# One attention visit per pair of heads instead of two, beside a feed-forward that holds TensorE

## The chip, the cores and the metric

The kernel runs on one core of a Trainium2 chip. The metric is the device time of one execution in microseconds (us); lower is better. A core has a matrix engine (TensorE, PE in the profile), a vector engine (VectorE, DVE), an activation engine (ScalarE, ACT), a general engine (GpSimd, POOL) and an engine that in this kernel only issues transfers (SyncE, SP). Each works through its own instructions in the order in which they were written; semaphores make one engine wait for another. Matmul results land in eight PSUM banks; all other tiles are in SBUF.

## The reference

Attention with normalised queries and keys, for 8 batches, 12 heads, 448 positions and 64 dimensions per head, and then a feed-forward on the 3584 tokens that come out of it:

```python
def rmsnorm(x, g):
    rms = np.sqrt(np.mean(x * x, axis=-1, keepdims=True) + 1e-06)
    return x / rms * g
q_n, k_n = (rmsnorm(q, g_q), rmsnorm(k, g_k))
scores = scale * np.matmul(q_n, k_n.transpose(0, 1, 3, 2))
scores = scores - np.max(scores, axis=-1, keepdims=True)
attn = np.exp(scores)
attn = attn / (np.sum(attn, axis=-1, keepdims=True) + 1e-09)
x = np.matmul(attn, v)            # then (B,H,S,D) -> (B*S, H*D) = (3584, 768)
h = np.maximum(x @ w_in, 0.0)     # w_in 768 x 2048
out = (h * h @ w_out)             # w_out 2048 x 768
```

All matmuls are in float32. The two weight matrices come in as 64-bit floats, and the kernel turns their words into float32 on the chip.

## The kernel before

**Pairs.** The 96 heads are worked through in 48 pairs, `i` = 0 to 47, six pairs for each batch. The two heads of a pair (`e` = 0 and 1) lie on partitions 0 to 63 and 64 to 127. The 448 keys of a head are cut into slots `m`: three of 128 keys, and the 64 last ones. The last keys of an even and an odd pair share one slot, `m == NJ` (3), which is computed with the even pair. So an even pair has four slots and an odd one three.

For each slot `weigh` (L378) makes the scores of both heads (L387, two matmuls on different halves of the array's rows, four for the shared slot) in two PSUM banks, and takes their exponentials on ScalarE (L392) into tiles `wT`, of which there are eight. `attend` (L446) multiplies a slot's exponentials by the values and accumulates in bank 4 (L455, two matmuls on different halves of the array's columns). The sums of the exponentials are added up on GpSimd (`additions`, L411) and brought over the partitions by one more pair of matmuls (`denominators`, L485), which writes the bank of `sums_bank` (bank 3 for these pairs); VectorE turns that bank (`take_sums`, L496), inverts (`invert`, L505 to L512) and multiplies bank 4 by it (`finish`, L524).

The queries and keys of a pair are loaded by `load_qk`, squared on ScalarE (L179), added up on VectorE (L192, L195), raised to the power -1/2 and scaled on GpSimd (`rescale`, L201 and L216), stored and loaded back in blocks of 32 by 32 (`store_q` L303, `load_blocks` L319), and transposed on VectorE (`turn_blocks`, L328, and L330 on ScalarE for the queries).

**Feed-forward.** Two batches make one pass `ffn(u)`, `u` = 0 to 3. Each product of halves is made by a seven-product scheme. A pass has four blocks. A block has two sets of seven first products (L643, six profile records of a 128x448 matmul for each product; ScalarE copies L650, VectorE adds L663, ScalarE squares L664 and L665), then the tokens left over (L695), then three sets of seven second products (L724, VectorE accumulates them, L765 and L741). Each product adds `COST_IN` (18) or `COST_OUT` (10) to `spent`; a block is 502, a pass (`COST`) 2008. A float32 matmul has two records in the profile.

**Order.** All engines follow an order written out by hand (`manual_schedule`). Pairs 0 to 12 run alone (`visit_alone`). From pair 13 on `run(until)` issues feed-forward products until `spent` reaches a mark, and `visit_among(i, n)` puts attention between them. A pair has two visits there:

- visit 0: the first two slots of the values of pair `i - 1`, then slots 0 and 1 of pair `i`;
- visit 1: the `denominators` and the other two slots of the values of pair `i - 1`, then the other slots of pair `i`.

In pass 0 (`first`) the `denominators` are put by themselves into the feed-forward, halfway between two visits. Small pieces of other work stand in two lists, `tasks` and `pool_tasks`; `run_tasks` takes one or two of each after every product, and all of them before a visit.

**Weights.** The 64 pieces of the weights are converted by `convert`: three ScalarE instructions (L825 to L827) on a tile `words`, of which there are three, and three VectorE ones (L838, L858, L862), then sums of pieces by VectorE and GpSimd in turn (L884). The first 16 pieces, for block 0, are converted beside the pairs that run alone. The other 48 are converted in pass 0, when `spent` reaches the entries of `late`: for block `b + 1`, eight pieces of `w_in` from halfway through block `b` on, and eight of `w_out` in the first half of block `b + 1`. Passes 1 to 3 load finished forms.

## Time and profile before

| | us |
|---|---|
| median of 5 runs | 1461.14 |
| lowest and highest of them | 1460.86, 1462.84 |
| the profiled execution's own time | 1461.48 |
| its span | 1459.7 |
| TensorE busy | 1425.5 |
| VectorE, ScalarE, GpSimd busy | 667.0, 583.7, 623.0 |

The span is the time from the first to the last instruction in the profile; 1.78 us of the profiled execution's time lie outside it. The stages follow the order above: pairs 0 to 12 alone until 147.4 us, pass 0 of the feed-forward with attention and conversion of weights until 511.6 us, passes 1 and 2 with attention until 1198 us, and then the rest of the feed-forward alone. Busy time of TensorE is a union of modelled spans, so a wait shorter than a matmul's drain does not show as idle time: distances between starts say more.

### The profile page before, as it was taken

The page shows a single profiled execution, that of the slowest core. Times are in us where ns is not written, and L with a number is a line of the kernel's source. Part 1 is how long each engine was busy: PE and PEld are TensorE (multiplying, and loading weights), DVE is VectorE, ACT ScalarE, POOL GpSimd, SP SyncE. Part 2 cuts the span into 40 slices and gives each one's busy share as a digit, 9 for nine tenths or more (in the row PEclk, how much of TensorE's full clock was granted, in tenths as well). Part 3 has the DMA queues.
Part 4 walks back from the last instruction along what each step waited for, and adds up shares of the span by engine and source line. Part 5 has one row for each costly group of instructions (what it writes and reads, how often), then busy time and mean ns, then how long its engine had stood idle before and what let it go on. Part 6 is the DMA issues. An engine that isn't in the chain of part 4 may idle for free.

```text
span 1459.7 us, 15299 instructions
## 1 busy us (share of the span) xinstructions
PE 1425.5 (98%) x4932; PEld 680.5 (47%) x4932; DVE 667.0 (46%) x1269; ACT 583.7 (40%) x1102; POOL 623.0 (43%) x522
## 2 busy tenths in 40 slices
PE   6989999999999999999999999999999999999998
PEld 2323444444444444445454544445444455555554
DVE  5877356786777623324342542324334251132313
ACT  6764455747555144432514234342332403222130
POOL 4545745655555635353543545245342422021111
PEclk9999999999999999999999999999999999999999
DMA  6565336666657554444435464334523223223122
GB/s 149 163 203 138 76 85 179 169 188 165 197 173 220 161 169 103 136 114 132 116 66 165 117 185 126 108 97 99 169 64 111 82 104 135 87 76 124 38 87 79
DMA packets 309278, 188.11 MB, mean 129 GB/s; under 512 B 265796, under 2 KB 293316, under 8 KB 300996
## 3 DMA queue, kind: packets, MB, share of 16 engines
q1 hardware_dynamic: 308384, 186.84, 43.7%
q8 instruction: 41, 0.67, 0.2%
q14 instruction: 49, 0.40, 0.1%
q10 hardware_dynamic: 804, 0.20, 0.1%
HBM read 144.57 MB, written 42.40 MB: 128 GB/s over the span
## 4 chain that ended last, share of the span: by engine, by line
PE 90%; DVE 4%; issue 2%; POOL 1%; ACT 1%; SPq 1%; DMA 0%; POOLq 0%; DVEq 0%
PE bank L643 35%; PE bank L724 29%; PE bank L455 9%; PE bank L387 8%; PE bank L695 5%; PE bank L485 2%; PE bank L468 1%; POOL rr L201 1%; DVE few L505 1%; DVE out_sb L884 0%; DMA qk<-in_k_dram 0%; DVE inverse L512 0%; DVE acc L765 0%; POOL qk L216 0%; POOL acc L181 0%
## 5 line engine op out<-in xcount | busy, mean ns | idle before, releaser
L643 PE MATMUL bank<-xT,in_sb 128*128 128x448 f32 x1344 | 517.5, 543 | 0.0
L643 PEld LDWEIGHTS bank<-xT,in_sb 128*128 128x128 f32 x1344 | 251.8, 190 | 262.3 <-issue 250.2
L765 DVE TENSOR_TENSOR acc<-acc,bank 128x384 f32<-128x384 f32 x324 | 173.7, 549 | 278.9 <-PE bank L724 205.6
L392 ACT ACTIVATE wT<-bank,rr 128x448 f32<-128x448 f32 x288 | 161.1, 631 | 268.9 <-PE bank L387 248.9
L201 POOL TENSOR_TENSOR rr<-ms,minus_half 128x16 f32<-128x16 f32 (+3 forms) x50 | 125.7, 2514 | 332.9 <-DVE ms L195 304.2
L724 PE MATMUL bank<-out_sb,hid 128*128 128x384 f32 x768 | 267.4, 488 | 0.0
L663 DVE TENSOR_TENSOR hid<-bank,part 128x448 f32<-128x448 f32 x128 | 76.8, 621 | 306.1 <-PE bank L643 306.1
L724 PE MATMUL bank<-out_sb,sums 128*128 128x384 f32 x576 | 204.0, 490 | 3.4 <-DVE acc L765 3.3
L724 PEld LDWEIGHTS bank<-out_sb,hid 128*128 128x128 f32 x768 | 144.9, 190 | 106.9 <-issue 6.8
L411 POOL TENSOR_TENSOR sum<-sum,wT 128x448 f32<-128x448 f32 (+1 forms) x144 | 164.2, 1163 | 12.8 <-ACT wT L392 10.4
L387 PE MATMUL bank<-qT,kT 64*128 64x448 f32 (+1 forms) x768 | 164.0, 573 | 3.7 <-ACT qT L330 1.6
L679 POOL TENSOR_TENSOR sums<-hid 128x384 f32<-128x384 f32 x32 | 32.8, 1024 | 291.5 <-ACT hid L665 291.0
L664 ACT ACTIVATE hid<-hid 128x448 f32<-128x448 f32 x128 | 73.2, 572 | 201.2 <-DVE hid L663 201.2
L724 PEld LDWEIGHTS bank<-out_sb,sums 128*128 128x128 f32 x576 | 107.7, 190 | 87.9 <-DVE acc L765 8.4
L650 ACT COPY part<-bank 128x448 f32<-128x448 f32 x128 | 67.7, 529 | 180.9 <-PE bank L643 180.8
L455 PE MATMUL bank<-wT,vt 128*64 128x448 f32 x480 | 106.3, 547 | 0.0
L387 PEld LDWEIGHTS bank<-qT,kT 64*128 64x128 f32 (+1 forms) x768 | 55.2, 173 | 108.8 <-issue 91.4
L411 POOL TENSOR_TENSOR sum<-wT 128x448 f32<-128x448 f32 x72 | 83.8, 1182 | 45.9 <-PE bank L485 45.9
L192 DVE TENSOR_REDUCE ms<-squares 128x8 f32<-128x512 f32 (+1 forms) x68 | 41.9, 616 | 124.7 <-ACT squares L179 124.7
L695 PE MATMUL bank<-out_sb,hid 128*128 128x384 f32 x256 | 86.4, 491 | 0.0
L665 ACT ACTIVATE hid<-hid 128x448 f32<-128x448 f32 x128 | 73.8, 577 | 4.0
L695 PEld LDWEIGHTS bank<-out_sb,hid 128*128 128x128 f32 x256 | 47.7, 190 | 39.3 <-issue 5.7
(83 smaller groups left out, 1126.4 us busy)
## 6 DMA issues: line engine op xcount, KB each, us to landing
out_sb<-out_forms SPq DMA_DIRECT2D x24, 1536.0 KB, 7.7
in_sb<-in_forms SPq DMA_DIRECT2D x24, 1344.0 KB, 6.0
words<-in_moe_w_in_dram SPq DMA_DIRECT2D x32, 384.0 KB, 3.6
words<-in_moe_w_out_dram SPq DMA_DIRECT2D x32, 384.0 KB, 3.7
out_forms<-out_sb SPq DMA_DIRECT2D x8, 1536.0 KB, 6.9
in_forms<-in_sb SPq DMA_DIRECT2D x8, 1344.0 KB, 5.5
qk<-in_q_dram SPq DMA_DIRECT2D x96, 96.0 KB, 3.1
vt<-in_v_dram SPq DMA_DIRECT2D x96, 96.0 KB, 3.3
```

The lines of the kernel that those rows point to most:

```text
L201: self.nc.gpsimd.tensor_tensor(out=self.rr[i][:, first : first + number, 0 : self.count(i)], in0=ms, in1=self.minus_half[:, :, None].to_br ...
L387: nc.tensor.matmul(sc[some], lhsT=turned[p, 1][r, keys], rhs=turned[p, 0][r, :], start=True, stop=True,)
L392: nc.scalar.activation(new_weights((i, m), e), sc, AF.Exp, scale=rows.rr[i][:, 1, 2 * m + e : 2 * m + e + 1],)
L411: nc.gpsimd.tensor_tensor(out=sums[i, e][some], in0=left[some], in1=weights[key_of(i, m), e][some], op=ALU.add)
L455: nc.tensor.matmul(banks[4][ds(e * D, D), 0:S], lhsT=lasts[i % 2][mine, e, :] if m == NJ else values[i][:, m, e, :], rhs=weights[key_of(i, ...
L643: nc.tensor.matmul(ps, lhsT=w_sb[:, IN.index(left), c, :], rhs=forms[u, c][right], start=first and c == 0, stop=c == NK - 1, skip_group_ch ...
L663: nc.vector.tensor_tensor(out=dst, in0=left, in1=right, op=op)
L664: nc.scalar.activation(dst, dst, AF.Relu)
L665: nc.scalar.activation(dst, dst, AF.Square)
L695: nc.tensor.matmul(ps, lhsT=flat[a][:, t, ds(NT * P, P)], rhs=w_sb[t][:, 2 * a + half, :], start=(a, t) == parts[0], stop=(a, t) == parts[-1],
L724: nc.tensor.matmul(ps, lhsT=lefts[left][:, t, ts(tt, P)], rhs=w_sb[t][:, OUT.index(right), :], start=first and t == 0, stop=t == 1, skip_g ...
L765: nc.vector.tensor_tensor(out=acc, in0=acc, in1=ps, op=ALU.add)
```

## The change

From pair 13 on each pair has one visit instead of two. Its order on TensorE: the scores of slots 0 and 1 of pair `i`; the four slots of the values of pair `i - 1`; the `denominators` of pair `i - 1` where they have not been made; the scores of the other slots of pair `i`. The exponentials of slots 0 and 1 are written between the value matmuls, since their tiles come free one slot at a time.

`weigh` is split into `score` (matmuls) and `weigh` (exponentials). The banks are dealt differently: slots 0 and 1 use banks 0 to 3, slot 2 banks 1 and 2, the shared slot banks 3 and 0, and the sums bank becomes bank 0. In pass 0 the `denominators` keep a place of their own, three quarters of the way from one visit to the next, and all waiting tasks are issued before them. Squares, normalisation and the turn through memory are made for pair `i + 3` instead of `i + 2`, so pair 12 prepares both 14 and 15; the transposes of pair `i + 1` and the loads of pair `i + 4` are put into `tasks` halfway before visit `i`. Pass 0 begins with five products ahead of pair 13's visit instead of two. The times of `late` change: pieces of `w_in` from 0.4 of block `b` on, 0.06 of a block apart, pieces of `w_out` from the start of block `b + 1` on, 0.055 apart.

The order of the instructions up to pair 11, and the number of matmuls, exponentials and transfers, stay as they are.

```diff
-    def weigh(i, m):
-
-        scs = [banks[m % 2 * 2 + e][:, 0:S] for e in range(2)]
+    def banks_of(i, m):
+
+        first = m % 2 * 2 if m < 2 or i <= 2 * NPAIR else 1 + (m - 2) * 2
+        return [banks[(first + e) % 4][:, 0:S] for e in range(2)]
+
+    def score(i, m):
+
+        scs = banks_of(i, m)
         for p in (i, i + 1) if m == NJ else (i,):
...
+    def weigh(i, m):
+
+        for e, sc in enumerate(banks_of(i, m)):
             nc.scalar.activation(
                 new_weights((i, m), e), sc, AF.Exp,
...
     def sums_bank(i):
-        return banks[5 if alone(i) else 3][:, 0:S]
+        return banks[5 if alone(i) else 0][:, 0:S]
...
     early = deque(2.4 * n for n in range(ahead + 1))
-    every = block / ahead
     late = deque(
-        block + 2 + every * (n - 2 * tile_pieces) for n in range(len(all_pieces) - ahead)
+        block * (n // ahead) + (0.4 * block + 0.06 * block * (n % ahead) if n % ahead < ahead // 2
+                                else block + 2 + 0.055 * block * (n % ahead - ahead // 2))
+        for n in range(len(all_pieces) - ahead)
     )
...
-    VISITS, last = 2, len(pairs) - 1
-    unit = 2 * NPAIR * VISITS
+    last, unit = len(pairs) - 1, 2 * NPAIR
...
     def visit_alone(i, n):
-        step = i * 2 * VISITS + 2 * n
+        later = (i + 2,) if alone(i) else (i + 2, i + 3)
+        step = 4 * i + 2 * n
...
-            square(i + 2, 0, new_acc())
-            square(i + 2, 1, new_acc(), nc.gpsimd)
+            for p in later:
+                square(p, 0, new_acc())
+                square(p, 1, new_acc(), nc.gpsimd)
...
-            normalize(i + 2)
+            for p in later:
+                normalize(p)
...
-    def visit_among(i, n):
+    def visit_among(i):
         run_tasks(len(tasks) + len(pool_tasks))
-        if not shift:
-            if n and i - 1 not in inverse:
+        if shift:
...
+        else:
+            if i <= last:
+                for m in slots_of(i, 0):
+                    score(i, m)
+            for n in range(NJ + 1):
+                attend(i - 1, (n,))
+                forget(i - 1, (n,))
+                if i <= last and n < 2:
+                    weigh(i, n)
+            if i - 1 not in inverse:
                 denominators(i - 1)
-            attend(i - 1, (2 * n, 2 * n + 1))
-            forget(i - 1, (2 * n, 2 * n + 1))
...
+            if i <= last:
+                weigh_slots(i, 1)
             tasks.append(lambda: invert(i - 1))
             tasks.append(lambda: finish(i - 1))
-        if n and i <= last and not shift:
-            additions(i)
...
+        if i <= last:
+            load_v(i)
+            if not shift:
+                additions(i)
+        if i + 3 <= last:
+            room = []
+            tasks.append(
+                lambda: room.append(io.tile([P, 4 * P], F32, name="squares", tag="squares", bufs=1))
+            )
+            for x in range(2):
+                tasks.append(lambda x=x: square(i + 3, x, room[0]))
+                tasks.append(lambda x=x: rows.add(i + 3, x))
+            tasks.append(lambda: pool_tasks.append(lambda: put_in_order(i + 3)))
...
+    def turn_among(i):
+        for x in (1, 0):
+            if in_blocks(i):
+                tasks.append(lambda x=x: turn_blocks(i, x))
...
         for i in range(len(pairs) + 1):
-            for n in range(VISITS):
-                at = i * VISITS + n - VISITS - unit
...
+            if i <= unit:
+                for n in range(2):
                     visit_alone(i, n)
-                    continue
...
+            u, x = divmod(i - unit - 1, unit)
+            if x == 0:
+                u, x = u - 1, unit
+            run(COST * (2 * x - 1) / (2 * unit))
+            if i < last and u >= 0:
+                turn_among(i + 1)
+            tasks.append(lambda i=i: load_qk(i + 4))
+            if first and u >= 0 and not shift:
+                run(COST * (4 * x - 1) / (4 * unit))
+                run_tasks(len(tasks) + len(pool_tasks))
+                denominators(i - 1)
+            run(COST * x / unit)
+            if x == unit:
+                drain()
+                stream, spent, first = ffn(u + 1), 0, u < 0
...
+                elif first:
+                    run(COST / (2 * unit))
+            visit_among(i)
+            if u < 0:
+                turn_among(i + 1)
```

## The prediction

> **What bounds the kernel now.** I read the page first (busy shares), then the table of stages, then TensorE's timeline in one stretch of each stage, then ScalarE's and VectorE's timelines where TensorE waits. Page, first part, and the table of stages (us from the start, PE, PEld, DVE, ACT, POOL busy, granted clock, DMA share, GB/s):
>
> ```profile
> PE 1425.5 (98%) x4932; PEld 680.5 (47%) x4932; DVE 667.0 (46%) x1269; ACT 583.7 (40%) x1102; POOL 623.0 (43%) x522
> 240.00:331.00 91.00, 88.61 (x294) 40.63 (x292) 71.50 (x120) 52.43 (x102) 51.84 (x40) 1.00 0.60 172
> 598.00:685.00 87.00, 87.00 (x299) 41.66 (x297) 32.66 (x64) 29.98 (x57) 38.71 (x32) 1.00 0.43 118
> ```
>
> TensorE is the bound: 98% busy, and from 511 us on it never idles; the clock is full. So only two things can shorten the span: less time per matmul, or the waits before 511 us, in pass 0, where VectorE is busy 71.5 of 91 us. The number of matmuls is the same. Time per matmul is not constant, as TensorE's timeline of the last stage (feed-forward alone) and of passes 1 and 2 shows (start, length, what, number of records):
>
> ```profile
> 1198.10 31.73 PE L643 MATMUL bank<-xT,in_sb 128*128 128x448 f32 x84
> 1229.67 5.32 PE L695 MATMUL bank<-out_sb,hid 128*128 128x384 f32 x16
> ...
> 699.80 11.54 PE L643 MATMUL bank<-xT,in_sb 128*128 128x448 f32 x30
> 711.27 0.97 PE L455 MATMUL bank<-wT,lasts 128*64 128x448 f32 x4
> 712.07 0.92 PE L455 MATMUL bank<-wT,vt 128*64 128x448 f32 x4
> 712.93 1.77 PE L387 MATMUL bank<-qT,kT 64*128 64x448 f32 x8
> 714.63 9.29 PE L643 MATMUL bank<-xT,in_sb 128*128 128x448 f32 x24
> 723.85 0.97 PE L485 MATMUL bank<-sum,ones 128*64 128x448 f32 x4
> 724.65 1.67 PE L455 MATMUL bank<-wT,vt 128*64 128x448 f32 x8
> 726.25 2.27 PE L387 MATMUL bank<-qT,kT 64*128 64x448 f32 x12
> ```
>
> From start to start, 84 uninterrupted records take 1229.67 - 1198.10 = 31.57 us, 0.3758 each. The 30 between two visits take 11.47, not 11.28: 0.20 over. The 24 take 9.22, not 9.02: 0.20 over. Two half-array matmuls run at once, so 8 value records should take 4 x 0.3758 = 1.50; they take 1.66: 0.15 over. 8 score records take 1.70: 0.20 over. Sums and values, both on halves of the columns, take 0.80 + 1.60 against 2.25: 0.15 over for both together. So **each stretch of one form costs 0.20 us (feed-forward, scores) or 0.15 us (values with or without sums), whatever its length**.
>
> **Part 1: fewer stretches.** Before, a pair has two stretches of each form: 2 x 0.20 + 2 x 0.20 + 2 x 0.15 = 1.10. After, scores, values with sums, scores, one feed-forward stretch: 0.20 + 0.15 + 0.20 + 0.20 = 0.75. That is 0.35 less, for the 35 pairs 13 to 47: 12.25. The visit behind the last pair has only values and sums, once instead of twice: 0.35 more. Pass 0 has sums by themselves 12 times instead of 11 (2.25 / 3 aside, such a stop costs 0.15 and one more feed-forward stretch, 0.20): 0.35 back. **Sum: 12.25 us.** One row is missing: feed-forward followed by scores. Nearest are feed-forward followed by values and scores followed by feed-forward (0.20 both), and transposes followed by scores or values (0.10); I take 0.20, which gives 12.25; with 0.10 it would be 15.75, with 0.25 10.5.
>
> [...]
>
> **Part 2: waits inside the visit.** Time from the visit's start, by the rows above: scores 0 to 1.70; values to 1.70 + 8 x 0.3758 + 0.15 = 4.85; with sums 5.60; then the other scores, into banks 1 and 2, which exponentials 2 and 3 must have read. An exponential of slot 0 needs its scores and one of the eight `wT` tiles, which the first value slot frees. ScalarE starts 1.1 us after the first start of what it waits for (scores at 626.86, exponentials at 627.97, four in 2.21), so at about 2.75; the third ends at 2.75 + 2 x 0.52 + 0.63 = 4.42. Slack: 1.1 us with sums in the visit (passes 1 and 2), 0.35 without (pass 0). Behind a late score stand all feed-forward products, in TensorE's order. For even pairs the shared slot also needs bank 0 after L496: sums end at 5.67, the transpose takes 0.64, the matmul comes at 6.45: nothing to 0.2 us each; I take 0. If VectorE had a backlog there, that would show 1:1.
>
> In passes 1 and 2 ScalarE is free in time (the nearest row before the visit, the square of the hidden values, ends 2.0 us into it), so I take no wait. In pass 0 three visits follow the tenth product of a block, with a conversion (L825) ahead of the exponentials in ScalarE's order. At the same place before, TensorE and ScalarE:
>
> ```profile
> 267.79 1.72 PE L455 MATMUL bank<-wT,vt 128*64 128x448 f32 x8
> ...
> 270.51 0.56 ACT L825 ACTIVATE words<-words 128x384 f32<-128x384 f32 x1 [4.05 <-DVE out_sb L884]
> 272.02 0.56 ACT L664 ACTIVATE hid<-hid 128x448 f32<-128x448 f32 x1
> 273.10 2.19 ACT L392 ACTIVATE wT<-bank,rr 128x448 f32<-128x448 f32 x4
> ```
>
> The exponentials start 5.31 us after the visit's start; in the next blocks 3.46 (361.13 - 357.67) and 4.16 (454.77 - 450.62). Before, nobody waited for them. After, that is 2.56, 0.71 and 1.41 over 2.75, less 0.35: 2.2 + 0.35 + 1.05 = 3.6 us. The changed order puts transposes (2 x 0.64), L496 and two joins (L838, L858, L862: 0.57 + 0.75 + 1.00) between the block's seventh and tenth product on VectorE, some 7.9 us with L884, after 1.35 us of adds, against 7.7 of TensorE; the tenth product's add is then 1.6 us late, which gives about 1.8 a visit, 5.4. I take **4.5** (0 to 9).
>
> **Part 3: waits of pass 0.** Before, TensorE waits at two places:
>
> ```profile
> 253.05 1.92 PE L387 MATMUL bank<-qT,kT 64*128 64x448 f32 x8
> 255.42 0.97 PE L387 MATMUL bank<-qT,kT 64*64 64x448 f32 x4 [0.45 <-ACT qT L330]
> ...
> 292.77 1.56 PE L724 MATMUL bank<-out_sb,sums 128*128 128x384 f32 x4 [0.68 <-DVE acc L765]
> 295.58 1.56 PE L724 MATMUL bank<-out_sb,sums 128*128 128x384 f32 x4 [1.25 <-DVE acc L765]
> ```
>
> The first: the shared slot needs the next pair's turned queries. From start to start these 12 records take 2.95, 3.27, 2.16, 3.52 and 3.26 us in pass 0, 1.87 where nothing is late: 5.8 us. After, the transposes are issued a quarter of a pair before the visit at the latest, from blocks loaded a pair earlier, and the shared slot comes 6 us into the visit: **5.8 us gone**; late next is what part 2 counts. The second: the 20 records of second products ahead of the visit take 9.01, 8.41 and 7.04 us instead of 6.54: 4.8 us. VectorE has more to do there than TensorE gives it time for, two conversions and their sums among it. The new `late` leaves about as many, and adds the two transposes and L496 for L511 to L524: I keep **4.8** (0 to 10). At the start, the sums of pair 13 come two products after its visit: six additions on GpSimd of 1.13 us end about when TensorE gets there: 0.3 (0 to 3).
>
> **Part 4: moved at no cost.** Pair 12 squares and scales pair 15 too: GpSimd 0.83 + 2.27 + 0.83 us; the first feed-forward products that need its T3 and T4 are the sixth and seventh, behind the visit of pair 13. SyncE: 9 more issues there (0.5 us each), all loads of q and k half a pair earlier, `load_v` behind the visit; each is used a pair (28 us) later and lands in 3.3. If a load came late, ScalarE's squares would hold up its copies (L650): up to some us once, in the range.
>
> **The sum.** Span 1459.7 - 12.25 - 5.8 - 4.8 + (4.5 + 4.8 + 0.3) = 1446.4. The profiled execution took 1461.48, 1.78 more than its span, and the median is 0.34 lower: 1446.4 + 1.78 - 0.34 = **1448**.
>
> **Rivals.** (A) Slower: the second scores wait for the exponentials of the first in every visit. For it: the chain scores, values, exponentials, scores exists only now, with 0.35 or 1.1 us of slack. Against it: exponentials start 2.77 after the visit in all passes 1 and 2. Price: each us beyond the slack is paid in 23 and 12 visits; it eats the 13 us of gain when the exponentials are 1.2 us late throughout. With the mean of the three rows above (4.31, 1.55 late): 23 x 0.45 + 12 x 1.2 = 25, less the 4.5 counted: about 1468. (B) Pass 0 gives it back: VectorE's bunches double the waits there, 9.6 more: 1458, hardly a change. For it: 71.5 of 91 us busy, and transposes, sums and conversions closer together; against it: as many instructions in as many microseconds. (C) Stretches cost nothing by themselves, so only part 3 moves: 1460. Against it: the 0.20 recurs in each of the rows above. (D) Pass 0 loses all its waits: 1438.
>
> **How the numbers follow.** Forecast (1441 to 1456) 0.70; A 0.09; B 0.09; C 0.04; D 0.08. Some 0.2% (2.9 us) is what a measurement of this kernel can tell from no change: faster means below 1458.2. D, the forecast and over half of B are faster: 0.84; C and the rest of B: 0.06; A and a worse B: 0.10. The range takes in the forecast, most of D and B: 1440 to 1459.
>
> **What would show it.** Right: between two visits of passes 1 and 2 one stretch of 60 records of L643 in about 22.75 us, a visit of some 7.2 us without gaps, a pass of about 341 us instead of 345; the shared slot's records at 1.87 in pass 0. Wrong: idle time before the second scores released by ScalarE (A), more time in the groups of L724 (B), feed-forward stretches of 60 records that cost more than 0.20 each (C).

## The result, and the profile after

| | before | after |
|---|---|---|
| median of the runs beside each other, us | 1461.42 (44 runs) | 1462.91 (24 runs) |
| span of the profiled execution | 1459.7 | 1460.6 |
| start of pass 0 | 147.42 | 146.88 |
| pass 0 | 360.8 | 372.7 |
| passes 1 and 2 | 689.9 | 679.4 |
| the rest, feed-forward alone | 261.6 | 261.6 |

The ratio is 1.0009, with a 95% interval of 1.0003 to 1.0014: no gain where 1448 was forecast, and above the forecast's range of 1440 to 1459. (Pass 0 is counted from its first product to the start of the visit that opens pass 1, at 508.23 before and 519.57 after; passes 1 and 2 from there to the first product of the last pass, at 1198.10 and 1198.99. The expectation of e1 below has 1199.15 for the last of these, and so 10.3 for 10.4.) Passes 1 and 2 became 10.4 us shorter, pass 0 11.9 us longer. Below, lines of the changed file are given: L652 was L643, L704 was L695, L733 was L724, L464 was L455, L393 was L387, L401 was L392, L494 was L485, L420 was L411, L673 and L674 (the squares of the hidden values) were L664 and L665, L834 to L836 (ScalarE's part of a conversion, called the split below; VectorE's part is the join) were L825 to L827, L774 was L765, L893 was L884. L304 and L310 are stores and L320 loads of the turn through memory, L157 and L166 load q and k, L815 loads words.

The page's first part, and the table of stages (same columns as before the change):

```profile
PE 1415.8 (97%) x4932; PEld 687.3 (47%) x4932; DVE 651.9 (45%) x1269; ACT 585.1 (40%) x1101; POOL 619.7 (42%) x523
```

```profile
240.00:331.00 91.00, 83.42 (x264) 38.98 (x261) 62.05 (x112) 51.43 (x101) 48.98 (x40) 0.96 0.59 172
598.00:685.00 87.00, 87.00 (x301) 42.81 (x300) 31.32 (x63) 31.43 (x58) 37.82 (x32) 1.00 0.43 119
```

In passes 1 and 2 (598 to 685 us) TensorE is still never idle. In 91 us of pass 0 it is now busy 83.4 us where it was 88.6, the other engines do less in the same time too, and the granted clock is 0.96 where it was 1.00.

TensorE's timeline in pass 1, from one visit to the end of the next:

```profile
525.39 22.82 PE L652 MATMUL bank<-xT,in_sb 128*128 128x448 f32 x60
548.13 1.77 PE L393 MATMUL bank<-qT,kT 64*128 64x448 f32 x8
549.84 0.97 PE L464 MATMUL bank<-wT,lasts 128*64 128x448 f32 x4
550.64 2.42 PE L464 MATMUL bank<-wT,vt 128*64 128x448 f32 x12
552.89 0.92 PE L494 MATMUL bank<-sum,ones 128*64 128x448 f32 x4
553.75 1.94 PE L393 MATMUL bank<-qT,kT 64*128 64x448 f32 x12
555.61 1.77 PE L652 MATMUL bank<-xT,in_sb 128*128 128x448 f32 x4
```

This is what the prediction described: 60 records in 22.74 us from start to start (60 x 0.3758 + 0.20 = 22.75), then a visit of 7.48 us with the shared slot, without a gap. Pass 0 is another matter. What TensorE waited for there, in all, number of times, longest:

```profile
PE bank L733 <- DVE acc L774: 6.5, 4, 4.5
PE bank L393 <- ACT wT L401: 4.9, 3, 1.9
PE bank L704 <- ACT hid L674: 2.5, 2, 1.3
PE bank L733 <- POOL out_sb L893: 1.0, 1, 1.0
PE bank L494 <- POOL sum L420: 0.3, 1, 0.3
```

Before, the same list was

```profile
PE bank L724 <- DVE acc L765: 3.3, 4, 1.3
PE bank L387 <- ACT qT L330: 1.6, 3, 0.7
```

That is 4.9 us; now it is 15.2. The shared slot's wait for `qT` is gone, as predicted; waits for exponentials, squares and accumulations have come.

**The longest wait, followed back.** TensorE, VectorE, ScalarE and SyncE's queue (SPq) behind the visit at 299.9 us:

```profile
316.03 1.45 PE L733 MATMUL bank<-out_sb,sums 128*128 128x384 f32 x4
322.01 5.71 PE L733 MATMUL bank<-out_sb,hid 128*128 128x384 f32 x12 [4.53 <-DVE acc L774]
```

```profile
320.74 0.55 DVE L192 TENSOR_REDUCE ms<-squares 128x6 f32<-128x384 f32 x1 [4.89 <-ACT squares L179]
321.33 0.17 DVE L195 TENSOR_SCALAR ms<-ms 128x6 f32<-128x6 f32 x1
321.41 0.55 DVE L774 TENSOR_TENSOR acc<-acc,bank 128x384 f32<-128x384 f32 x1
```

```profile
308.98 0.57 ACT L836 ACTIVATE words<-words 128x384 uint32<-128x384 f32 x1
318.75 0.55 ACT L834 ACTIVATE words<-words 128x384 f32<-128x384 f32 x1 [9.20 <-DMA words<-in_moe_w_in_dram]
...
320.20 0.51 ACT L179 ACTIVATE squares<-qk 128x384 f32<-128x384 f32 x1
```

```profile
299.51 0.39 SPq L815 DMA_DIRECT2D words<-in_moe_w_in_dram  x1
299.94 2.74 SPq L304 DMA_DIRECT2D q_rows<-qk  x1
302.72 2.25 SPq L310 DMA_DIRECT2D q_rows<-qk  x2
307.90 1.90 SPq L320 DMA_DIRECT2D qk<-q_rows  x4
309.84 1.01 SPq L157 DMA_DIRECT2D qk<-in_q_dram  x2
310.89 1.34 SPq L166 DMA_DIRECT2D qk<-in_q_dram  x2
312.27 1.12 SPq L157 DMA_DIRECT2D qk<-in_k_dram  x2
313.44 1.26 SPq L166 DMA_DIRECT2D qk<-in_k_dram  x2
314.80 0.54 SPq L815 DMA_DIRECT2D words<-in_moe_w_in_dram  x1
```

Read from the bottom: SyncE issues the words of one piece at 299.51 and those of the next only at 314.80, behind the stores and loads of the attention. ScalarE reaches the split (L834) at 309.5 and stands there for 9.2 us. The squares of a coming pair (L179) are behind the split, VectorE's reduction (L192) waits for the squares, the accumulation (L774) is behind the reduction, and TensorE's next product needs the bank that this accumulation frees. In pass 0 neither TensorE's matmuls nor VectorE, ScalarE or GpSimd wait for a load of q and k itself; the one that comes late is the load of words behind them (ScalarE waits 23.2 us for words there, 9.2 of them in this place).

**Half the clock.** The 12 records at 322.01 take 5.55 us from start to start (327.56 - 322.01), where 12 such records without a wait take 3.87. The granted clock, in a table of stages with short windows:

```profile
270.00:274.00 4.00, 2.47 (x12) 0.78 (x8) 2.31 (x6) 3.85 (x9) 0.72 (x1) 1.00 0.76 219
274.00:277.40 3.40, 3.40 (x5) 1.51 (x5) 0.00 (x0) 1.11 (x2) 3.32 (x4) 0.50 1.10 428
277.40:281.00 3.60, 3.60 (x11) 1.87 (x10) 0.27 (x1) 1.99 (x4) 2.62 (x3) 1.00 0.19 79
318.00:321.80 3.80, 0.00 (x0) 0.00 (x0) 1.03 (x3) 2.40 (x5) 0.00 (x0) 1.00 1.11 382
321.80:325.20 3.40, 3.19 (x5) 1.83 (x6) 3.23 (x9) 0.43 (x2) 1.77 (x1) 0.50 0.70 255
325.20:329.00 3.80, 3.80 (x14) 1.96 (x13) 3.32 (x6) 1.18 (x3) 2.48 (x4) 1.00 0.83 188
```

Three stretches of 3.41 us have clock 0.50. They start at 274.02, 321.81 and 373.01 us: 1.29 us behind the wait of 1.53 us that ends at 272.73, at the end of the one of 4.53 us that ends at 322.01, and 1.70 us behind the one of 1.52 us that ends at 371.31. Half of 3.41 us is 1.71, so each costs up to that much of matmul time (the 12 records above lost 1.68), 5.1 us together. Behind the wait of 1.88 us that ends at 466.22 the clock is 1.00 (460 to 475 us). In pass 0 of the kernel before there is none; its longest wait was 1.25 us, and the clock from 147 to 508 us 1.00.

**The balance of pass 0.** For each stretch of one form, the excess is the distance from its start to the next one's, less the records at their undisturbed rate (0.3758 us for L652, 0.3225 for L704 and L733, 0.188 for half-array ones), less the cost of the stretch by the prediction's rows: 0.20, or 0.15 for values (with or without sums) and for sums alone; the shared slot's scores are taken at 1.87 in all. Where second products follow first ones directly, 0.20 is taken off for both, though they are 0.10 and 0.09 over (in pass 1, 24 first products' records from 555.61 to 564.74 us and 36 behind them until 576.44); this happens at four places of the changed pass 0 and at none before, so the excess of the changed kernel is really 0.8 more. Summed over pass 0, in us:

| excess at | before | predicted | after |
|---|---|---|---|
| scores and values (the visits) | 5.8 | 4.5 | 7.4 |
| sums | 0 | 0.3 | 1.1 |
| first products | 0 | 0 | 2.5 |
| second products and leftover tokens | 4.8 | 4.8 | 13.8 |
| together | 10.6 | 9.6 | 24.8 |
| of it by half clock | 0 | 0 | 5.1 |

### The profile page after: what moved, and what is told of

It is laid out like the page before. It is cut to its first block, busy times and chain, and to the rows that moved or that the text cites. A ratio compares the mean times of both kernels' runs of the same rounds, so it can differ in the third digit from the quotient of the medians.

```text
span 1460.6 us, 15312 instructions
## 1 busy us (share of the span) xinstructions
PE 1415.8 (97%) x4932; PEld 687.3 (47%) x4932; DVE 651.9 (45%) x1269; ACT 585.1 (40%) x1101; POOL 619.7 (42%) x523
## 4 chain that ended last, share of the span: by engine, by line
PE 86%; DVE 5%; ACT 3%; DMA 3%; POOL 2%; issue 1%; SPq 0%; DVEq 0%; ACTq 0%; POOLq 0%
PE bank L652 32%; PE bank L733 28%; PE bank L464 9%; PE bank L393 8%; PE bank L704 5%; PE bank L494 2%; DMA words<-in_moe_w_in_dram 1%; PE bank L477 1%; DVE few L514 1%; DMA words<-in_moe_w_out_dram 1%; ACT hid L674 1%; ACT hid L673 1%; ACT words L834 1%; POOL sum L420 0%; POOL rr L201 0%
## 5 line engine op out<-in xcount | busy, mean ns | idle before, releaser
L652 PE MATMUL bank<-xT,in_sb 128*128 128x448 f32 x1344 | 516.1, 543 | 0.0
L652 PEld LDWEIGHTS bank<-xT,in_sb 128*128 128x128 f32 x1344 | 254.1, 191 | 260.5 <-issue 251.8
L733 PE MATMUL bank<-out_sb,hid 128*128 128x384 f32 x768 | 269.3, 489 | 6.7 <-DVE acc L774 5.7
L774 DVE TENSOR_TENSOR acc<-acc,bank 128x384 f32<-128x384 f32 x324 | 174.4, 551 | 222.3 <-PE bank L733 186.0
L401 ACT ACTIVATE wT<-bank,rr 128x448 f32<-128x448 f32 x288 | 160.6, 634 | 155.7 <-PE bank L393 85.9
L733 PE MATMUL bank<-out_sb,sums 128*128 128x384 f32 x576 | 204.5, 490 | 0.8 <-DVE acc L774 0.8
L733 PEld LDWEIGHTS bank<-out_sb,hid 128*128 128x128 f32 x768 | 145.9, 191 | 112.6 <-DVE acc L774 9.3
L420 POOL TENSOR_TENSOR sum<-wT 128x448 f32<-128x448 f32 x72 | 81.0, 1146 | 245.4 <-PE bank L494 187.2
L393 PE MATMUL bank<-qT,kT 64*128 64x448 f32 (+1 forms) x768 | 161.3, 578 | 6.0 <-ACT wT L401 4.9
L420 POOL TENSOR_TENSOR sum<-sum,wT 128x448 f32<-128x448 f32 (+1 forms) x144 | 160.9, 1144 | 2.8
L673 ACT ACTIVATE hid<-hid 128x448 f32<-128x448 f32 x128 | 73.3, 573 | 195.9 <-DVE hid L672 195.9
L733 PEld LDWEIGHTS bank<-out_sb,sums 128*128 128x128 f32 x576 | 107.8, 190 | 84.9 <-issue 6.8
L393 PEld LDWEIGHTS bank<-qT,kT 64*128 64x128 f32 (+1 forms) x768 | 54.6, 174 | 104.4 <-issue 61.2
L464 PE MATMUL bank<-wT,vt 128*64 128x448 f32 x480 | 99.6, 544 | 0.0
L505 DVE STREAM_TRANSPOSE inverse<-bank 128x448 f32<-128x448 f32 x48 | 30.7, 640 | 131.9 <-PE bank L494 114.9
L704 PE MATMUL bank<-out_sb,hid 128*128 128x384 f32 x256 | 86.0, 487 | 2.5 <-ACT hid L674 2.5
L331 ACT ACTIVATE qT<-qT,g 128x448 f32<-128x448 f32 x34 | 22.7, 667 | 152.3 <-DVE qT L329 152.3
L674 ACT ACTIVATE hid<-hid 128x448 f32<-128x448 f32 x128 | 73.8, 577 | 4.0
```

What stands on the lines that cost most here:

```text
L393: nc.tensor.matmul(sc[some], lhsT=turned[p, 1][r, keys], rhs=turned[p, 0][r, :], start=True, stop=True,)
L401: nc.scalar.activation(new_weights((i, m), e), sc, AF.Exp, scale=rows.rr[i][:, 1, 2 * m + e : 2 * m + e + 1],)
L420: nc.gpsimd.tensor_tensor(out=sums[i, e][some], in0=left[some], in1=weights[key_of(i, m), e][some], op=ALU.add)
L464: nc.tensor.matmul(banks[4][ds(e * D, D), 0:S], lhsT=lasts[i % 2][mine, e, :] if m == NJ else values[i][:, m, e, :], rhs=weights[key_of(i, ...
L652: nc.tensor.matmul(ps, lhsT=w_sb[:, IN.index(left), c, :], rhs=forms[u, c][right], start=first and c == 0, stop=c == NK - 1, skip_group_ch ...
L673: nc.scalar.activation(dst, dst, AF.Relu)
```

## The experiments

The theory was that pass 0 gives the gain back because the 48 conversions, the attention's preparation and the visits now meet in the in-order engines. Its rivals: the new times in `late` alone are at fault; the visits by themselves are (without conversions the loss stays); the words come late, by a missing tile or by SyncE's order. All results first; the times are medians, excess and half clock (1.71 us for each 3.41 us at clock 0.50) are those of pass 0 in the profiled execution. That execution can lie some us from the median (e7 2.7 below, e18 2.1 below, e16 3.1 above), and the five runs of e17, for one, spread from 1453.05 to 1456.97, so differences of 2 or 3 us in excess between two kernels say little by themselves. e3, e4, e13, e14 and e17 leave work out and do not compute the reference.

| run | us | ratio to before (95%) | excess | of it half clock |
|---|---|---|---|---|
| e1 old times of `late` | 1462.82 | 1.0012 (1.0002 to 1.0021) | 25.1 | 6.8 |
| e2 new times in the kernel before | 1470.74 | 1.0071 (1.0054 to 1.0088) | 18.6 | 3.4 |
| e3 no conversions | 1442.73 | 0.9874 (0.9857 to 0.9890) | 3.9 | 0 |
| e4 the same before | 1453.39 | 0.9953 (0.9936 to 0.9969) | 2.2 | 0 |
| e5 conversions behind the visit | 1459.90 | 0.9989 (0.9980 to 0.9999) | 22.4 | 6.8 |
| e6 loads behind the visit | 1459.18 | 0.9987 (0.9978 to 0.9997) | 19.0 | 3.4 |
| e7 sums in the visit | 1458.36 | 0.9982 (0.9972 to 0.9991) | 22.3 | 1.7 |
| e8 four words tiles | 1480.99 | 1.0132 (1.0115 to 1.0149) | 22.5 | 3.4 |
| e9 e6 and e7 | 1463.31 | 1.0011 (1.0002 to 1.0020) | 29.7 | 6.8 |
| e10 e5, e6 and e7 | 1456.69 | 0.9970 (0.9958 to 0.9983) | 22.5 | 5.1 |
| e11 e6 and e7, old times | 1475.60 | 1.0105 (1.0090 to 1.0121) | 40.9 | 13.7 |
| e12 words by GpSimd | 1501.54 | 1.0277 (1.0263 to 1.0291) | 61.1 | 18.8 |
| e13 words not loaded | 1454.99 | 0.9951 (0.9937 to 0.9964) | 16.6 | 3.4 |
| e14 the same before | 1461.46 | 1.0000 (0.9991 to 1.0009) | 10.4 | 0 |
| e15 e5 and e7 | 1452.79 | 0.9947 (0.9934 to 0.9961) | 18.2 | 3.4 |
| e16 e5 and e6 | 1454.20 | 0.9944 (0.9931 to 0.9958) | 17.7 | 3.4 |
| e17 e15, words not loaded | 1456.62 | 0.9954 (0.9941 to 0.9968) | 22.8 | 6.8 |
| e18 e15, `w_in` later | 1450.46 | 0.9920 (0.9906 to 0.9933) | 14.9 | 1.7 |

### The times of `late` (e1, e2)

e1 puts the old list into the changed kernel, e2 the new list into the kernel before:

```diff
+    every = block / ahead
     late = deque(
-        block * (n // ahead) + (0.4 * block + 0.06 * block * (n % ahead) if n % ahead < ahead // 2
-                                else block + 2 + 0.055 * block * (n % ahead - ahead // 2))
-        for n in range(len(all_pieces) - ahead)
+        block + 2 + every * (n - 2 * tile_pieces) for n in range(len(all_pieces) - ahead)
     )
```

> The changed kernel with the old times of late. Known so far: passes 1 and 2 became 10.3 us shorter (1198.10 - 508.23 = 689.9 to 1199.15 - 519.57 = 679.6), pass 0 with its visits 11.9 us longer (360.8 to 372.7). Theory 1 (the one visit and what is issued around it put the transfers of q and k ahead of the words of the weights in SyncE's order, and ScalarE and VectorE stand behind them; the times of late matter little): within 4 us of the changed kernel, 1459 to 1466. Theory 2 (the new times of late bunch the conversions): pass 0 falls to about 358, 1446 to 1452. Theory 3 (VectorE and ScalarE have too much to do between visits that lie farther apart, whatever the conversions): no change, 1461 to 1464.

> The kernel before with the new times of late alone. Theory 1: within 3 us of before, 1458 to 1464. Theory 2: slower by about what pass 0 lost, 1469 to 1475. Theory 3: within 3 us of before.

In the changed kernel the list makes no difference to the time (1462.82 against 1462.91): the values' excess falls from 5.1 to 0.7, and that at second products rises from 13.8 to 21.8. In the kernel before, the new list costs 9.9 us (1470.74 against 1460.86 in the runs beside it), with 10.5 of excess at scores and 4.4 at first products. e1 lies where theories 1 and 3 put it, e2 where theory 2 did, so none of the three holds for both. The times alone don't explain the loss; they decide where it falls.

### Without conversions (e3, e4)

The 48 conversions of pass 0 are replaced by plain loads of the same number of bytes as a finished piece, in both kernels.

```diff
     def load_weights(n):
-        if n >= len(all_pieces) or moe_w_in.dtype == F32:
+        if n >= ahead or moe_w_in.dtype == F32:
             return
...
         else:
-            nc.sync.dma_start(dst, rows)
+            flat = q_all[0].rearrange("h s d -> (h s d)").rearrange("(p n) -> p n", p=P)
+            nc.sync.dma_start(dst, flat[:, ds(n % 7 * HALF, HALF)])
```

> The changed kernel without the conversion of the 48 pieces of pass 0: no words, no ScalarE and VectorE instructions on them; each piece is one load of float32 numbers from q in place of the weights, so the output is not the reference's. Sums of pieces and stores of forms stay. Theories 1 and 2: the waits of pass 0 go nearly all, and against the kernel before with the same left out it is 12 to 18 us faster; about 1435 to 1442. Theory 3: the waits in the visits and in the second products of pass 0 stay, and it is at most 5 us faster than the kernel before with the same left out.

> The kernel before with the same left out as in e3 (the conversion of the 48 pieces of pass 0; loads of q in place of weights). By all theories 1447 to 1457: of its 10.6 us of waits in pass 0 the 4.8 at the second products go, and perhaps the 5.8 at the shared slot. It is the measure for e3.

Without conversions the changed kernel beats the one before by 10.7 us (1442.73 against 1453.39), and the excess of pass 0 falls to 3.9. Theories 1 and 2 had 12 to 18 us for this difference, theory 3 at most 5: it lies between, nearer to the first. Conversions cost 20.2 us in the changed kernel and 7.5 in the one before (1460.86 beside it). So what the visits and stretches were to bring is there; the conversions take it back.

### Conversions, loads and sums moved by one place each (e5, e6, e7)

e5 keeps a conversion that falls due at a visit behind the visit's first product; e6 issues the loads of pair `i + 4` behind visit `i`; e7 makes the sums of pass 0 in the visit, without a stop of their own that first issues all waiting tasks.

```diff
-            while first and late and late[0] <= spent:
+            while first and late and late[0] <= spent < until:
```

```diff
-            tasks.append(lambda i=i: load_qk(i + 4))
...
             visit_among(i)
+            tasks.append(lambda i=i: load_qk(i + 4))
```

```diff
-            if first and u >= 0 and not shift:
-                run(COST * (4 * x - 1) / (4 * unit))
-                run_tasks(len(tasks) + len(pool_tasks))
-                denominators(i - 1)
```

> The changed kernel, but a conversion that falls due with the last product ahead of a mark (a visit, the sums, the transposes) waits for the first product behind it. Known: with the conversions left out the change gains 10.7 us (1453.4 to 1442.7), with them it loses 1.5, so they cost the changed kernel 20 us and the one before 7.5. In the changed trace 7 us of this are inside the three visits behind a tenth product (values 1.6, 1.6, 1.95 us over their rate, second scores 0.6, 1.1, 0.5). If these come from the conversion ahead of the exponentials in ScalarE's order: the 7 us fall below 2, and the time by 4 to 7, to 1455 to 1459. If they come from VectorE's late add alone (the square ahead of the exponentials waits for it): they stay above 4, and the time within 3 us of 1462.8.

> The changed kernel with the loads of q and k of pair i + 4 put into the tasks behind visit i instead of halfway before it. In the changed trace the load of words behind the visit at 299.9 us is issued at 314.8, behind stores, waits and 12 loads of q and k in SyncE's order, and the second products there wait 6.6 us; in the next block 2.4. Theory 1 (SyncE's order delays the words): these 9 us shrink by 3 to 7, to 1456 to 1460. Rival (VectorE alone is too slow there): no change, 1461 to 1465.

> The changed kernel with the sums of pass 0 inside the visit, as in passes 1 and 2, without a stop and a flush of the tasks of their own. The 12 stops cost 0.35 us each by the rows, 4.2 together, and the second scores get 0.75 us more slack in 12 visits. If the flush ahead of the sums is what bunches VectorE's and SyncE's work: 8 to 12 us faster than the changed kernel, 1451 to 1455. If not: 4 to 6 us, 1457 to 1459.

e5: the visits' excess falls from 7.4 to 3.7, the first products' from 2.5 to 0, and second products rise from 13.8 to 17.6. Conversions ahead of the exponentials make about half of the visits' waits, as the prediction said; more than half of what is saved comes up elsewhere, and the time gains 3.0 us where 4 to 7 were expected. e6: the chain shown above is gone. The same products on TensorE's timeline, without a wait:

```profile
316.87 1.45 PE L733 MATMUL bank<-out_sb,sums 128*128 128x384 f32 x4
318.16 4.14 PE L733 MATMUL bank<-out_sb,hid 128*128 128x384 f32 x12
322.14 1.45 PE L733 MATMUL bank<-out_sb,sums 128*128 128x384 f32 x4
```

and the words are issued 4 us earlier on SyncE, with a shorter row of loads ahead:

```profile
300.35 0.38 SPq L815 DMA_DIRECT2D words<-in_moe_w_in_dram  x1
300.78 1.00 SPq L304 DMA_DIRECT2D q_rows<-qk  x1
301.83 3.19 SPq L310 DMA_DIRECT2D q_rows<-qk  x2
308.71 1.90 SPq L320 DMA_DIRECT2D qk<-q_rows  x4
310.71 0.42 SPq L815 DMA_DIRECT2D words<-in_moe_w_in_dram  x1
```

These 48 second products lose 0.3 us instead of 6.6, and all second products 6.8 instead of 13.8. So the place of these loads, which the prediction had moved "at no cost", made that wait; VectorE being too slow there, the rival, is out. But one visit of block 3 now waits 4.2 us, and only 3.7 us of the time remain gained. e7 gains 4.6 us, about what 12 stops cost by the rows (4.2): that the flush of tasks ahead of the sums bunches the work is not shown by it.

### A fourth words tile (e8)

```diff
-        words[n] = ffn_p.tile([P, HALF, 2], U32, name="words", tag="words", bufs=3)
+        words[n] = ffn_p.tile([P, HALF, 2], U32, name="words", tag="words", bufs=4)
...
-        return ffn_p.tile([P, S], F32, name="part", tag="part", bufs=4)
+        return ffn_p.tile([P, S], F32, name="part", tag="part", bufs=3)
...
-        return ffn_p.tile([P, S], F32, name="xT", tag="xT", bufs=11 * NK - 1)
+        return ffn_p.tile([P, S], F32, name="xT", tag="xT", bufs=31)
```

> The changed kernel with four tiles for the words instead of three; to make room xT has 31 instead of 32 and part 3 instead of 4. A load of words then need not wait for VectorE's join of the piece three before it, but stands where it stood in SyncE's order. If that wait for a free tile is what makes words late: 6 to 12 us faster than the changed kernel, 1451 to 1457. If SyncE's order is: within 4 us. The smaller xT and part can only cost.

The 18 us lost lie in the stage of pairs alone, which ends 20.7 us later, perhaps because the room for the fourth tile was missing there; that part says nothing of the question. In pass 0 the excess is 22.5 instead of 24.8, and the 48 products behind the visit still lose 6.2. A free words tile is not what was late.

### Pairs and triples of the moves (e9, e10, e11), and the words by another queue (e12)

e9 has the edits of e6 and e7, e10 those of e5, e6 and e7, e11 those of e9 and e1. e12 is the changed kernel with

```diff
+        queue = nc.sync if n < ahead + 2 else nc.gpsimd
         if kind == "in":
-            nc.sync.dma_start(
+            queue.dma_start(
```

> The changed kernel with both edits of the two earlier runs: the loads of q and k of pair i + 4 are issued behind visit i, and in pass 0 the sums are made inside the visit. Theory (pass 0 loses by several waits with separate causes, one at transfers issued ahead of the words, one at stops of the order for the sums): the two gains add up, 3.7 + 4.6 us less than the changed kernel, about 1454.5, excess in pass 0 about 16. Rival (one backlog on VectorE and ScalarE that comes out wherever TensorE next depends on them): the second edit brings nothing over the first, about 1458.

> As the run before, and a conversion that falls due with the last product ahead of a visit waits for the first product behind it. Separate waits: the visits' waits (about 4 us of values) go down too, about 1451. One backlog: what the visits save comes back in second products, within 1 us of the run before.

> As the first run of this call, with the times of late that the kernel before has. If the places of the conversions matter little beside the other two edits, within 1.5 us of the first run of this call; if the new times are what let the visits run, 3 us or more slower; if they are a cost as in the kernel before (9.9 us there), 3 us or more faster.

> The changed kernel, but the words of the pieces from the eighteenth on are loaded through GpSimd's queue, not SyncE's. Theory that the words stand behind stores and loads of the attention on SyncE (words issued at 299.51 and the next at 314.80): the waits of ScalarE's L834 for words become shorter, the 48 second products behind the visit lose their 6.6 and 2.4 us, about 1455. Rival that the transfers themselves are slow or that the tile comes free late: no change, 1463 +- 1.5. If GpSimd's own work is held up by its issues: slower, its additions late for the sums, some 3 to 10 us more.

e9 is a miss for the sum of the two: each gained about 4 us, together they lose 0.4. One reason is the clock: 6.8 us lost by half clock instead of 3.4 in e6 and 1.7 in e7; and the visits' excess is 14.6 us (e6 9.7, e7 6.2). e10, with conversions behind the visits, is 6.6 us better than e9, which is neither "about 1451" nor "within 1 us", and e11, with the old times, 12.3 worse, with 13.7 us lost by half clock. So beside the other edits the times matter a great deal, where e1 had shown no difference: what one of these edits brings depends on the others. e12 is the worst run: 38.6 us slower than the changed kernel, with waits for accumulations (10.3 us), for exponentials (11.9) and for what GpSimd computes (8.8). It shows that the words were not better off there, not that SyncE was without blame.

### Words without their transfers (e13, e14)

```diff
+        if n >= ahead:
+            words[n] = kept[n % 3]
+            return
         kind, t, form, rows = all_pieces[n]
-        words[n] = ffn_p.tile([P, HALF, 2], U32, name="words", tag="words", bufs=3)
+        words[n] = kept[n % 3] = ffn_p.tile([P, HALF, 2], U32, name="words", tag="words", bufs=3)
```

> The changed kernel; the conversions of pass 0 work on three words tiles that were loaded for block 0, so the 48 loads of words in pass 0 are left out (the weights of blocks 1 to 3 are other numbers), and all instructions of ScalarE, VectorE and GpSimd stay. Theory that late words hold up ScalarE and what stands behind its splits: most of the 20 us that the conversions cost goes, 1443 to 1450, excess in pass 0 below 13, and the 48 second products behind the visit near 0. Rival that the instructions themselves (48 x 4 us on ScalarE and VectorE, in order with the attention's) make the waits: within 3 us of the changed kernel, 1460 to 1463.

> The same in the kernel before. Conversions cost it 7.5 us in all. Theory of late words, which the change brought: little of that goes, 1459 to 1461. Rival: if loads of words cost the kernel before as much as the changed one, both gain alike.

This separates the transfers from the instructions. In the changed kernel 7.9 us go (1462.91 to 1454.99), in the kernel before nothing (1461.46). Second products fall from 13.8 to 6.0, and the visits' excess stays, 7.2 for 7.4. In the list of waits of pass 0, the same two rows as above, 4.9 and 6.5 in the changed kernel, are in e13

```profile
PE bank L393 <- ACT wT L401: 4.5, 3, 1.5
PE bank L733 <- DVE acc L774: 1.4, 3, 0.8
```

The time lies between what the theory (1443 to 1450) and the rival (1460 to 1463) had, so each is right in part. Of the 12.7 us by which conversions cost more than before (20.2 less 7.5), about 8 came with the words' transfers (1.7 of them one stretch at half clock less); that the words' place in the queue does it, and not the transfers as such, is what e6 shows, which leaves all of them in and takes 7.0 us from the same second products. The waits in the visits come from the instructions: they stay here, and fall to 0.6 in e3.

### Towards a better order (e15, e16, e17, e18)

e15 has the edits of e5 and e7, e16 those of e5 and e6. e17 is e15 with the edit of e13. e18 is e15 with

```diff
-        block * (n // ahead) + (0.4 * block + 0.06 * block * (n % ahead) if n % ahead < ahead // 2
+        block * (n // ahead) + (0.56 * block + 0.05 * block * (n % ahead) if n % ahead < ahead // 2
```

> The changed kernel with the sums of pass 0 inside the visit, and conversions due at a visit put behind its first product; loads of q and k as in the changed kernel. If the edits add up: 1458.4 - 3.0 = 1455.4, excess in pass 0 about 18. If the first of them only fills what the second opens: 1458 +- 1.

> The changed kernel with the loads of q and k of pair i + 4 behind visit i, and conversions due at a visit put behind its first product; sums as in the changed kernel. If the edits add up: 1459.2 - 3.0 = 1456.2, with the visits' waits halved and the 48 second products near 1.5. If not: 1459 +- 1.

> The kernel of e15 with the words of pass 0 not loaded (conversions work on three words tiles of block 0; the weights of blocks 1 to 3 are other numbers). If its 14.8 us at second products, of which L704 waits 5.8 for ScalarE's squares, come from splits that wait for words ahead of those squares: excess in pass 0 below 9 and 1444 to 1447. If they come from the instructions alone: within 2 us of 1452.8.

> The kernel of e15 with pieces of w_in converted from 0.56 of a block on, 0.05 of a block apart, in place of 0.4 and 0.06, so that none falls among the last first products and the leftover tokens (L704). If conversions at that place hold up the squares that L704 needs: its 12.3 us in three stretches of 36 second products fall to about 4, and the time to 1444 to 1449. If the pieces, closer together, only wait for words later, or come late for the next block's first products: 1452 to 1458, with excess at the 64 second products or the first products.

e15 and e16 add up and gain more than the sum of their parts: in e15 the visits wait for exponentials hardly at all (excess of scores and values 1.3 instead of 7.4). But with the sums' stop gone, in e15 as in e7, e9, e10, e11, e17 and e18, the visit of pair 14 waits 2.5 us for its queries. Most of what is left in e15 is at L704, on ScalarE and TensorE:

```profile
284.86 0.57 ACT L834 ACTIVATE words<-words 128x384 f32<-128x384 f32 x1 [1.50 <-DMA words<-in_moe_w_in_dram]
...
287.48 0.58 ACT L674 ACTIVATE hid<-hid 128x448 f32<-128x448 f32 x1
```

```profile
289.18 2.93 PE L704 MATMUL bank<-out_sb,hid 128*128 128x384 f32 x4 [2.90 <-ACT hid L674]
```

Splits and joins of `w_in` pieces stand ahead of the squares that the leftover tokens need. e17 is a miss: without the words' transfers the median is 3.8 us longer, not shorter, though the runs of the two overlap (1453.05 to 1456.97 and 1452.34 to 1455.91). In the profiled executions 3.4 of it is the clock (6.8 us against 3.4), and without it the excess is 16.0 against 14.8; TensorE now waits 6.0 us for sums of pieces on GpSimd. So late words were not what was left in e15. e18 then moved the pieces away from L704, and the waits there are gone:

```profile
281.50 5.32 PE L704 MATMUL bank<-out_sb,hid 128*128 128x384 f32 x16
286.66 2.74 PE L733 MATMUL bank<-out_sb,hid 128*128 128x384 f32 x8
```

The three stretches of 36 (16 records of leftover tokens and 20 of second products) lose 4.6 us instead of 12.3, as expected, and the stretches of 64 second products 6.3 instead of 2.3; that the pieces are denser there may be why. The expected time, 1444 to 1449, was missed by 1.5. e18 takes 1450.46 us, the fastest of all complete kernels: 0.9920 (0.9906 to 0.9933) of the kernel before. What it still waits for, by the waits of pass 0:

```profile
PE bank L733 <- DVE acc L774: 4.0, 7, 1.1
PE bank L733 <- POOL out_sb L893: 3.9, 3, 2.1
PE bank L393 <- ACT qT L331: 2.5, 1, 2.5
```

## Why the prediction was wrong

**The step that failed is the term for second products in part 3, "I keep 4.8 (0 to 10)".** It measured 13.8, and 2.5 more came at first products, for which no term stood. The argument was a count: the new `late` leaves "about as many" instructions to VectorE. The count was right (VectorE has 1269 instructions in both), but it says nothing of what stands ahead of what. e13 and e6 show what took its place: 7 to 8 of the 9.0 us more at second products came because ScalarE, in its order, stood at words that had not come, with the squares and so VectorE's accumulations behind it. The largest single case is the 6.6 us of the 48 second products from 306.65 on.

**Part 4 failed with it.** The moved loads of q and k were priced by whether they land in time for their own use; they do, as neither TensorE's matmuls nor VectorE, ScalarE or GpSimd wait for one in pass 0. The price was paid by the words issued behind them on SyncE. The sentence "if a load came late, ScalarE's squares would hold up its copies" had the mechanism, with the wrong load.

**The clock.** "The clock is full" was taken to stay so, since the trace of before showed 1.00 beside waits of up to 1.25 us. It didn't: 5.1 us in pass 0, which were in no term and no rival (they are counted within the excesses above).

**Part 1 was right.** Its share for passes 1 and 2 was 8.4 us (24 x 0.35); they became 10.4 shorter. The rows assumed for feed-forward and scores hold (0.20). Of the 2.0 more, 1.3 is the shared slot, whose 12 records take 1.87 instead of a mean of 1.99 us in each of 11 even pairs, which no term had; 0.75 is only the border of the stages, since the sums of pair 24 (four records) now lie in pass 0. The whole change without conversions is worth 10.7 us (e3 against e4).

**Part 2** was right in place and kind, and its size, 4.5 (0 to 9), measured 7.4; half clock behind two of these waits (from 274.02 and 373.01 us on) makes nearly all of the 2.5 at first products besides. The visits of passes 1 and 2 wait for nothing, so rival A's mechanism is not there; in pass 0 it is, in the three visits that part 2 named. **Part 3's** first item was right: the shared slot takes 1.87 us in pass 0 where nothing disturbs it, and the 5.8 us are gone. Sums cost 1.1 instead of 0.3, all of it at pair 13, where the products ahead of them take 0.3 more.

**The sum**: the span is 14.2 us over the forecast. Waits of pass 0 rose by 15.0 (24.8 and 0.8 less 10.6) where 1.0 less was forecast, 16.0 over; the shared slots of passes 1 and 2 gave 1.3, and the start 0.5. Pass 0's stretches saved the 3.85 that part 1 gives them: 15.0 less 3.85, and 0.75 more for the sums of pair 24, is the 11.9 by which pass 0 grew. Rival B had the place and about the size right, 9.6 us more waits than forecast where it became 16.0, and was given 0.09. Its mechanism, bunches on VectorE, is not what the runs show for the larger part: e6 moves only loads and takes half of the second products' excess away, and in the table of stages VectorE was busy 62.05 of 91 us where it had been 71.50. Against B stood "as many instructions in as many microseconds", the argument that failed.

**What stays open.** Why two moves that each gain can lose together (e9) is explained only in part, by the 6.8 us lost by half clock. What makes the waits that are left at second products without the words' transfers (6.0 us in e13, 14.8 in e17) is not separated further.

## What to carry to other kernels

Where several engines work in order and one of them waits for a transfer, a moved transfer is priced by what stands behind it in its queue, and then by what stands behind the waiting instruction on the engine that needs it, not by its own deadline; the same count of instructions in about the same time cost 10.6 us of waits here in one order and 24.8 in another. In such a stage the effects of single moves need not add up, so their places are tried in combination, and each version is read by its waits per place as well as by its total. And keep the stops of TensorE short: here three of 1.52 to 4.53 us came with half clock that cost up to 1.71 us on top of each, and those in pass 0 of the kernel before, of up to 1.25 us, with none.

## What the runs showed of the hardware

In pass 0 some stops of TensorE had a stretch at a granted clock of 0.50 (half clock) beside or behind them, and some had not:

- In the kernel before, the waits of pass 0 last up to 1.25 us, and the clock is 1.00 from 147 to 508 us. Among the pairs that run alone it is 0.52 from 77.50 to 80.90 us.
- In the changed kernel three stretches of 3.41 us have clock 0.50, at the waits of 1.53, 4.53 and 1.52 us; at the wait of 1.88 us the clock is 1.00. The 12 records of second products from 322.01 us on, with clock 0.50 for their first 3.21 us, took 5.55 us instead of 3.87 (308.05 to 311.92).
- In e15, behind the start of a wait of 2.90 us that ends at 289.18, the clock is 0.51 from 288.40 to 291.90 us and 0.50 from there to 295.30.
- The wait of 2.5 us for the queries of pair 14 went both ways. Behind it the clock is 0.50 in e9 and e11 (181 to 183 us) and in e10 (179 to 181), and 0.62 on average from 179 to 183 us in e17; in e7, e15 and e18 it is 1.00 from 175 to 191 us.

What decides whether half clock follows a stop, and below which length of a stop it does not, is not shown by these runs.
